# Scores of the first units moved to other PSUM banks, and the opening's instruction list rewritten around it

## The chip, the cores and the metric

The kernel runs on one core of a Trainium2 chip. The metric is the time of one execution on the device, in microseconds (us); lower is better. The engines are PE (matrix multiply), DVE (vector), ACT (scalar, activation functions), POOL (GpSimd) and SP, which here only starts DMA transfers. Each engine takes its own instructions in the order in which they were issued.

## What is computed

Windowed attention feeds a feed-forward layer whose gate is a softmax. The inputs are `q`, `k`, `v` of 8 batches, 8 heads, 576 positions and 64 columns, in fp32:

```python
scores = q @ k.T / 8
# heads 0-3: the last 32 positions; heads 4-7: every 4th of the last 128
scores = where(mask, scores, -1e9)
attn = exp(scores - max); attn /= sum(attn) + 1e-9
x = (attn @ v) as (4608 tokens, 512)
h = x @ w_in                       # 512 -> 1024
solu = h * softmax(h)
ln = (solu - mean) / sqrt(var + 1e-6) * g_ln
out = ln @ w_out                   # 1024 -> 512
```

`w_in` and `w_out` arrive as fp64 and are turned into fp32 on the chip.

## The kernel before

**Attention** works on 32 units n, each a pair of heads of one batch. `q` and `v` load a unit. `S` makes the scores: two matmuls that put the mask down and 80 small ones (lines 203, 211). Then `max`, `sub`, `exp`, `sum`, `inv`, `norm` make the softmax (lines 237 to 268), `turn` transposes it on DVE (L273), `V` multiplies with v (L289), and `xh`, `xl` split the result into two parts of reduced precision, `x_hi` and `x_lo` (L314, L328; on POOL, L322, a copy `xc`, L318, comes out of PSUM first). `sub` is on DVE (L247) straight out of PSUM, except for the units in `ACT_SCORES`: there ACT copies the scores out (`cp`, L241) and POOL subtracts (L250). `norm` runs on POOL for the units in `POOL_NORM`, else on DVE (both L268); `xl` runs on POOL for the units in `POOL_X`.

**The feed-forward part** works on 36 tiles i of 128 tokens. The product h is made in four quarters of 6 matmuls, `ha hb hc hd` (L341): `ha` and `hb` give the first 512 columns, `hc` and `hd` the second, and `ha`, `hc` need the first half of the 512 inputs (the first two units of a batch), `hb`, `hd` the others. Then `peak` (DVE, L352), `e` (ACT, L359), `gate` (DVE, L366), `mid` (ACT for tiles in `ACT_CENTRE`, L379, else DVE, L382) and `var` (ACT and six small POOL instructions). `forth` and `back` carry the tile through DRAM, `trA trB` transpose on DVE (L455), `thA thB` (ACT) and `tlA tlB` (POOL, L468) split it, `o` multiplies with `w_out` (24 matmuls, L477), and `out` scales and stores.

**The weights** come in 16 parts b, 0 to 7 of `w_in` and 8 to 15 of `w_out`: `w` loads one (512 KB), `abs` and `low` (ACT), `clamp` (DVE, L519), `sign` (DVE, L526) and `join` (DVE, L534) build the fp32 number, `gain` scales it (`w_out` only), `hi` (ACT, L544) and `lo` (L548) split it; `lo` is on DVE for the parts in `DVE_LOW`, else on POOL. `ha` needs parts 0 and 2, `hc` 1 and 3, `hb` 4 and 6, `hd` 5 and 7.

**PSUM** is one tensor of 8 banks of 512 columns. h of tiles 0 and 2 lies in banks 0 and 1, h of all other tiles in banks 2 and 3, `o` in bank 0 or 1, the result of `V` in columns 0 to 143 of banks 4 to 7. Scores of units below `MERGED` lie in banks 2 and 3, those of the others in columns 144 to 463 of banks 6 and 7. Waits are derived by the framework from what each instruction reads and writes.

**The order** is written out by hand: `OPENING` is one list of words, each word issues one step, and it reaches to tile 7 and unit 11. After it a loop issues the words of `STEP` for each tile. An engine's queue is the list's words that belong to it, in the list's order. SP's words are `w q v ib m g i forth back`. A transfer into a buffer waits for the last reader of what was there (`w7` for `sign0`, `q4` for S0, `v6` for V2).

PE's order in the opening before: S0 S1 S2 V0 S3 V1 S4 V2 ha1 hc0 V3 ha0 hb0 S5 hd0 hc1 V4 hb1 hd1 S6 ha2 hc2 V5 hd2 hb2 hc3 S7 ha3 hb3 hd3 V6 S8 hc4 V7 ha4 hd4 hb4 S9 o0 hc5 ha5 hd5 hb5 o1 V8 and so on.

Of the kernel before, what the change touches and what calls it, by code (L numbers as in the profile page):

```python
# [28 lines left out]
WQ = 2 * WIN  # L29
NG = P // WIN  # L30
GQ = S // NG
NS = -(-GQ // WIN)
# [4 lines left out]
SIGN_BIT = -(1 << 31)  # L37
PE_MASK = (0, 1, 2, 3, 4, 5, 6, 7, 8, 9)
POOL_SUB = True
POOL_NORM = (0, 1, 2, 3, 4, 5, 6, 7, 8, 9)  # L40
ACT_SCORES = (1, 5, 7, 8, 9)
POOL_X = (0, 4, 5)
DVE_LOW = (12, 13, 14, 15)
ACT_CENTRE = (0, 1, 2, 3, 4)
Q_BUFS, V_BUFS, T_BUFS, TH_BUFS, CONV_BUFS = 4, 4, 4, 2, 4
REBIAS = 2.0**16
F64_MIN = REBIAS * float(np.array(0x38000000, np.uint32).view(np.float32))
F64_MAX = REBIAS * float(np.array(0x47EFFFFF, np.uint32).view(np.float32))
FIRST = 6
OPENING = (  # L50
# [25 lines left out]
)  # L76
STEP = (
    "back.j trA.k thA.k trB.k thB.k tlA.k tlB.k ha.i hb.i S.n q.n mask.n max.n sub.n hc.i hd.i "
# [8 lines left out]
BY_PE = "t.i th.i tl.i".split()  # L87
LAST = NTILE - 1
SLOTS = "t0 t1 t2 t3 raw4 raw5 tp t0 t1 t2 t3 raw4 raw5 tp t3 tp".split()
MERGED = 5  # L90
SHIFT = {"th0": 88}


# [1 line left out]
def windowed_attention_then_solu_kernel(  # L95
# [41 lines left out]
    banks = psum.tile([P, 8, 512], F32, name="banks")  # L137
# [8 lines left out]

    def ps_s(n):
        if n < MERGED:
            return banks[:, 2:4, 0 : NS * WQ]
        return banks[:, 6:8, GQ : GQ + NS * WQ]  # L150

    nc.vector.memset(mhalf, -0.5)
# [41 lines left out]
    def scores(n):  # L194

        qt, kt = loaded[n]["q"], loaded[n]["k"]
        dil = int(n % NPAIR >= NPAIR // 2)
        ps = ps_s(n)
        st[n] = {"ps": ps.rearrange("p h (s w) -> p h s w", w=WQ)}
        on_pe = n in PE_MASK  # L200
        if on_pe:
            for h in range(2):
                nc.tensor.matmul(  # L203
                    out=ps[:, h, :], lhsT=id_bf, rhs=mask_sb[:, dil, :],
                    start=True, stop=False, skip_group_check=True,
                )
        for i in range(NS):
            for h in range(2):
                for c in range(NG):
                    q0 = GQ * c + WIN * i  # L210
                    nc.tensor.matmul(  # L211
                        out=ps[WIN * c : WIN * c + WIN, h, WQ * i : WQ * i + WQ],
                        lhsT=qt[D * h : D * h + D, q0 : q0 + WIN],
                        rhs=kt[D * h : D * h + D, q0 : q0 + WQ],
                        start=not on_pe,
                        stop=True,
                        skip_group_check=True,
                    )

    def soft_mask(n):  # L220
        if n in PE_MASK:
            return
        dil = int(n % NPAIR >= NPAIR // 2)
        sm = st[n]["sm"] = att.tile([P, 2, NS, WQ], F32, name=f"sm{n % 2}")
        nc.vector.tensor_tensor(  # L225
            out=sm.rearrange("p h s w -> p h (s w)"), in0=ps_s(n),
            in1=mask_sb[:, dil, :].unsqueeze(1).broadcast_to([P, 2, NS * WQ]),
            op=ALU.add,
        )

    def wide(x):
        return x.unsqueeze(3).broadcast_to([P, 2, NS, WQ])
# [10 lines left out]
    def soft_sub(n):  # L243
        mx = st[n]["mx"]
        if n in PE_MASK and n not in ACT_SCORES:
            sm = st[n]["sm"] = att.tile([P, 2, NS, WQ], F32, name=f"sm{n % 2}")
# [18 lines left out]
    def soft_norm(n):  # L265
        sm, rs = st[n]["sm"], st[n]["rs"]
        eng = nc.gpsimd if n in POOL_NORM else nc.vector
        eng.tensor_tensor(out=sm, in0=sm, in1=wide(rs), op=ALU.mult)  # L268
# [51 lines left out]
    def spread_lo(n):  # L320
        if n in POOL_X:
            nc.gpsimd.tensor_tensor(  # L322
                out=x_part(n, x_lo), in0=st[n]["x"], in1=x_part(n, x_hi).bitcast(F32),
                op=ALU.subtract,
            )
            del st[n], loaded[n]
            return
        nc.vector.tensor_tensor(  # L328
            out=x_view(n, x_lo), in0=from_v(n), in1=x_view(n, x_hi).bitcast(F32), op=ALU.subtract
        )  # L330
        del st[n], loaded[n]
# [39 lines left out]
    def moe_centre(i):  # L371
        src, dst, mu = ms[i]["t"], ms[i]["t"], ms[i]["mu"]
        if not by_dma(i):
            ms[i]["t"] = moe.tile([P, DF], F32, name="tp", bufs=1)
            dst = ms[i]["t"].rearrange("p (k j s) -> p k j s", j=NG, s=WIN)
            src = src.rearrange("p (j k s) -> p k j s", j=NG, s=WIN)
        if i in ACT_CENTRE:
            nc.vector.tensor_scalar(out=mu, in0=mu, scalar1=-1.0 / DF, scalar2=None, op0=ALU.mult)
# [167 lines left out]
    def conv_lo(b):  # L546
        eng = nc.vector if b in DVE_LOW else nc.gpsimd
        eng.tensor_tensor(  # L548
            out=w_part(b)[:, 1, :], in0=cv[b]["mag"], in1=hi(b).bitcast(F32), op=ALU.subtract
        )  # L550
        del cv[b]
# [30 lines left out]
    for i in range(FIRST, NTILE + 2):  # L582
        of = {"n": fronts.get(i), "m": fronts.get(i - 1), "i": i, "j": i - 1, "k": i - 2}
        words_of = {LAST: LAST_STEP}.get(i, STEP)
        for word in (words_of if i <= LAST else "o.k out.k").split():
            name, which = word.split(".")
            n = of[which]
# [78 lines left out]
```

## Time and profile before

| what | value |
|---|---|
| runs shown | 519.17, 519.04, 516.50 us (median 519.04) |
| profiled execution | 515.99 us, of which the span from first to last instruction is 514.2 |
| granted clock of PE | 0.998 |
| busy: PE, DVE, ACT, POOL | 482.4, 343.0, 235.2, 218.5 us |
| first matmul of h | 40.65 us |
| DMA | 88.37 MB, mean 172 GB/s |

In the profile's lists a line such as L341 is the line of the kernel that issued the instruction; "x12" is a count; "[1.66 <-DVE x_lo L328]" says that the engine stood idle for 1.66 us and that the DVE instruction of line 328 which writes `x_lo` ended it. The stretches give, for each engine, busy microseconds in that stretch and the number of instructions. Neighbouring instructions of one engine overlap a little in the records, so the chain, which cuts them to what follows on, gives the shorter and better durations.

### The profile page before, as it was taken

What the parts mean: (1) busy time and instruction counts of PE and PEld (TensorE: products, weight loads), DVE (VectorE), ACT (ScalarE), POOL (GpSimd) and SP (SyncE); (2) the same over time, 40 slices, a digit from 0 to 9 for tenths busy, and PEclk for the clock granted to TensorE, in tenths of its full rate; (3) what the DMA queues carried; (4) which work ended last, traced back from release to release, by engine and by line L of the source; (5) the groups of instructions that cost most, each with busy time, mean ns of one, the idle gap of its engine ahead of it and who ended that gap; (6) DMA issues with size and microseconds to landing.
All of it is one profiled execution on the core that took longest, in us unless ns stands there. A gap on an engine that the chain in (4) does not pass through costs nothing.

```text
span 514.2 us, 16377 instructions
## 1 busy us (share of the span) xinstructions
PE 482.4 (94%) x7132; PEld 388.2 (75%) x7132; DVE 343.0 (67%) x539; ACT 235.2 (46%) x387; POOL 218.5 (42%) x342
## 2 busy tenths in 40 slices
PE   1359989999999999999999999999999999999997
PEld 1237767788788888888888888888877888888885
DVE  3999999766467765577677766576677776444540
ACT  3857888633344443344433344343434444333351
POOL 1634775634444443444434443444444334333360
PEclk9999999999999999999999999999999999999999
DMA  7969186636585664556655564646644333333331
GB/s 274 402 234 376 46 286 197 197 125 212 169 273 184 184 180 137 153 183 182 182 169 172 181 182 137 183 154 184 177 141 134 105 106 91 111 108 103 108 98 61
DMA packets 47304, 88.37 MB, mean 172 GB/s; under 512 B 5504, under 2 KB 23808, under 8 KB 47232
## 3 DMA queue, kind: packets, MB, share of 16 engines
q1 hardware_dynamic: 47232, 87.32, 53.2%
q8 instruction: 56, 0.92, 0.7%
q14 instruction: 16, 0.13, 0.1%
HBM read 59.51 MB, written 27.79 MB: 170 GB/s over the span
## 4 chain that ended last, share of the span: by engine, by line
PE 90%; DMA 4%; DVE 3%; SPq 1%; issue 0%; ACT 0%; ACTq 0%; DVEq 0%
PE banks L341 40%; PE banks L477 39%; PE banks L289 6%; PE banks L211 5%; DMA raw<-w_in 1%; DMA kt<-kT 1%; DMA qt<-qT 1%; DVE low L526 1%; DVE pt L273 0%; DVE mag L534 0%; DVE rs L258 0%; PE banks L203 0%; DVE sm L247 0%; DVE mx L237 0%; SPq L165 0%
## 5 line engine op out<-in xcount | busy, mean ns | idle before, releaser
L341 PE MATMUL banks<-w_i,x_hi 128*128 128x512 f32 x576 | 183.1, 399 | 0.5 <-DVE mu L366 0.4
L477 PE MATMUL banks<-w_o,th 128*128 128x512 f32 x576 | 181.0, 395 | 0.0
L341 PEld LDWEIGHTS banks<-w_i,x_hi 128*128 128x128 f32 x576 | 106.6, 190 | 24.6 <-DVE mu L366 1.0
L477 PEld LDWEIGHTS banks<-w_o,th 128*128 128x128 f32 x576 | 106.2, 188 | 22.1 <-DVE w_o L548 0.2
L341 PE MATMUL banks<-w_i,x_lo 128*128 128x512 f32 x288 | 113.0, 393 | 0.0
L477 PE MATMUL banks<-w_o,tl 128*128 128x512 f32 x288 | 112.2, 390 | 0.0
L468 POOL TENSOR_TENSOR tl<-t,th 128x512 fp32r<-128x512 f32 x70 | 89.7, 1299 | 41.1 <-ACT th L463 41.1
L352 DVE TENSOR_REDUCE nmax<-banks 128x1 f32<-128x1024 f32 x36 | 44.0, 1223 | 65.2 <-PE banks L341 65.2
L254 ACT ACTIVATE sm<-sm 128x640 f32<-128x640 f32 x32 | 23.5, 736 | 94.5 <-POOL sm L250 94.0
L359 ACT ACTIVATE e<-banks,nmax 128x1024 f32<-128x1024 f32 x36 | 40.2, 1117 | 51.4 <-DVE nmax L352 50.8
L341 PEld LDWEIGHTS banks<-w_i,x_lo 128*128 128x128 f32 x288 | 54.5, 189 | 11.7
L477 PEld LDWEIGHTS banks<-w_o,tl 128*128 128x128 f32 x288 | 54.1, 188 | 11.7
L387 ACT ACTIVATE e<-t 128x1024 f32<-128x1024 f32 x35 | 37.2, 1062 | 55.2 <-DVE t L382 55.2
L366 DVE CUSTOM_DVE_ANT_0 t<-banks,e 128x1024 f32<-128x1024 f32 x36 | 43.9, 1219 | 17.1 <-ACT e L359 17.0
L289 PEld LDWEIGHTS banks<-pt,vt 32*64 32x64 f32 x2816 | 34.8, 138 | 18.9 <-issue 11.3
L463 ACT CAST th<-t 128x512 fp32r<-128x512 f32 x70 | 41.7, 619 | 15.9 <-DVE t L455 8.6
L455 DVE STREAM_TRANSPOSE t<-raw 128x512 f32<-128x512 f32 x70 | 44.9, 677 | 3.8 <-issue 2.6
L225 DVE TENSOR_TENSOR sm<-banks,mask_sb 128x640 f32<-128x640 f32 x22 | 18.1, 824 | 44.0 <-PE banks L211 43.8
L250 POOL TENSOR_TENSOR sm<-sm,mx 128x640 f32<-128x640 f32 x27 | 34.5, 1276 | 29.7 <-DVE mx L237 26.7
L289 PE MATMUL banks<-pt,vt 32*64 32x64 f32 (+3 forms) x2816 | 38.1, 234 | 7.7 <-DVE pt L273 7.7
L392 POOL TENSOR_SCALAR sq<-sq 128x1 f32<-128x1 f32 x36 | 7.7, 215 | 86.1 <-ACT e L387 85.6
L388 POOL TENSOR_SCALAR se<-se 128x1 f32<-128x1 f32 x36 | 8.7, 243 | 77.3 <-ACT e L359 76.6
(62 smaller groups left out, 474.7 us busy)
## 6 DMA issues: line engine op xcount, KB each, us to landing
mid<-t SPq DMA_DIRECT2D x140, 128.0 KB, 2.3
raw<-mid SPq DMA_DIRECT2D x35, 512.0 KB, 3.5
vt<-vw SPq DMA_DIRECT2D x32, 384.0 KB, 4.0
kt<-kT SPq DMA_DIRECT2D x32, 312.0 KB, 4.2
qt<-qT SPq DMA_DIRECT2D x32, 296.0 KB, 4.6
out<-ob SPq DMA_DIRECT2D x36, 256.0 KB, 2.1
t<-w_in SPq DMA_DIRECT2D x5, 512.0 KB, 7.2
t<-w_out SPq DMA_DIRECT2D x4, 512.0 KB, 6.7
```

Source lines behind the costliest of these rows:

```text
L211: nc.tensor.matmul(out=ps[WIN * c : WIN * c + WIN, h, WQ * i : WQ * i + WQ], lhsT=qt[D * h : D * h + D, q0 : q0 + WIN], rhs=kt[D * h : D * ...
L250: eng.tensor_tensor(out=st[n]["sm"], in0=st[n]["sm"], in1=wide(mx), op=ALU.subtract)
L289: nc.tensor.matmul(out=ps_x[D * h : D * h + D, c, c0 : c0 + k1 - k0], lhsT=vt[WIN * c : WIN * c + WIN, i, D * h : D * h + D], rhs=pt[WIN * ...
L341: nc.tensor.matmul(out=ps_h(i)[:, half], lhsT=a[:, kt, xs], rhs=w_i[:, kt, half, part, :], start=(kt == 0 and k == 0), stop=(kt == KT - 1 ...
L352: nc.vector.tensor_reduce(out=nmax, in_=h, axis=AX.X, op=ALU.max, negate=True)
L359: nc.scalar.activation(out=e, in_=h, func=AF.Exp, bias=nmax, scale=1.0, accum_out=se)
L366: nc.vector.tensor_tensor_reduce(out=t, in0=h, in1=ms[i]["e"], scale=1.0, scalar=0.0, op0=ALU.mult, op1=ALU.add, accum_out=mu,)
L387: nc.scalar.activation(out=e, in_=t, func=AF.Square, accum_out=sq)
L455: nc.vector.transpose(out=turned(i)[:, cut(c)].rearrange("p k (a r) -> p k a r", r=WIN), in_=ms[i]["mv"].rearrange("p (a k s) -> p k a s", ...
L463: nc.scalar.copy(out=ms[i]["th"][:, cut(c)], in_=turned(i)[:, cut(c)])
L468: nc.gpsimd.tensor_tensor(out=ms[i]["tl"][:, cut(c)], in0=turned(i)[:, cut(c)], in1=ms[i]["th"][:, cut(c)].bitcast(F32), op=ALU.subtract,)
L477: nc.tensor.matmul(out=ps_o(i), lhsT=a[:, f, :], rhs=w_o[:, f, part, :], start=(f == 0 and k == 0), stop=(f == FT - 1 and k == 2),)
```

## The change

`MERGED` goes from 5 to 4, and the units below it no longer share one pair of banks: units 0 and 2 keep banks 2 and 3, units 1 and 3 use banks 0 and 1. Unit 4 joins the later units in banks 6 and 7.

The lists that share work among engines change, and so does the whole opening list, which keeps all steps that it had but for a few at its far end that the loop issues instead.

```diff
-POOL_NORM = (0, 1, 2, 3, 4, 5, 6, 7, 8, 9)
-ACT_SCORES = (1, 5, 7, 8, 9)
-POOL_X = (0, 4, 5)
-DVE_LOW = (12, 13, 14, 15)
-ACT_CENTRE = (0, 1, 2, 3, 4)
+POOL_NORM = (0, 1, 2, 3, 4, 5, 6, 7)
+ACT_SCORES = (5, 6, 9)
+POOL_X = (1, 4, 5, 6)
+DVE_LOW = (7, 9, 11, 12, 15)
+ACT_CENTRE = (0, 1, 2, 4, 5)
...
-    "w1 ib abs1 w3 m0 low1 q0 clamp1 w0 sign1 w2 abs3 q1 low3 q2 join1 hi1 S0 sign3 clamp3 "
-    "join3 hi3 w4 low0 max0 sub0 m1 sign0 abs0 w5 S1 clamp0 abs2 low2 w8 exp0 lo1 join0 clamp2 "
...
+    "ib m0 q0 w1 S0 low1 q1 w2 max0 w0 m1 abs1 sub0 exp0 low2 low0 q2 sign1 clamp1 w5 sum0 w3 "
+    "abs2 v1 S1 abs0 inv0 join1 v0 hi1 max1 norm0 sub1 exp1 abs3 clamp2 sign2 turn0 low3 sum1 "
+    "lo1 inv1 sign0 join2 S2 w4 clamp0 clamp3 abs5 sign3 join3 q3 V0 q4 max2 S3 sub2 clamp5 "
+    "norm1 hi3 join0 w6 xh0 turn1 exp2 xl0 lo3 hi2 V1 sum2 hi0 low5 inv2 low4 lo0 low6 v2 abs4 "
+    "sign4 sign5 clamp4 join4 join5 max3 w7 norm2 w8 xc1 xh1 xl1 low7 sub3 turn2 S4 exp3 lo2 "
+    "hi5 q6 sum3 inv3 abs7 abs6 max4 hc1 w12 sub4 norm3 sign6 V2 ha0 hi4 clamp6 w9 join6 hc0 "
...
-MERGED = 5
+MERGED = 4
...
         if n < MERGED:
-            return banks[:, 2:4, 0 : NS * WQ]
+            return banks[:, 2:4, 0 : NS * WQ] if n % 2 == 0 else banks[:, 0:2, 0 : NS * WQ]
         return banks[:, 6:8, GQ : GQ + NS * WQ]
```

On SP the new list starts ib m0 q0 w1 q1 w2 w0 m1 q2 w5 w3 v1 v0 w4 q3 q4 w6 v2 w7 w8 q6 w12 w9 w10 v3 g v5 v4 v6 w11 q5 v7 w14 q7 forth0 q9 back0 forth1 w13 q8 v8 back1 w15 forth2.

PE's order in the new opening: S0 S1 S2 V0 S3 V1 S4 hc1 V2 ha0 hc0 V3 ha1 hb0 S5 hd0 hd1 V4 hb1 S6 hc2 ha2 hb2 V5 hd2 S7 hc3 ha3 V6 hb3 hd3 V7 S8 ha4 hc4 hb4 hd4 S9 hc5 hd5 ha5 hb5 o0 o1 ha6 hc6 hb6 hd6 V8 and so on.

DVE's order in the new opening up to its fifth `gate`: max0 sub0 sign1 clamp1 sum0 inv0 join1 max1 sub1 clamp2 sign2 turn0 sum1 inv1 sign0 join2 clamp0 clamp3 sign3 join3 max2 sub2 clamp5 join0 turn1 xl0 sum2 inv2 sign4 sign5 clamp4 join4 join5 max3 sub3 turn2 sum3 inv3 max4 sub4 sign6 clamp6 join6 clamp7 turn3 xl2 sum4 sign7 join7 clamp10 xl3 inv4 sign10 lo7 join10 clamp8 max5 peak0 turn4 sign11 sign8 gate0 sum5 inv5 peak1 max6 clamp11 join11 turn5 gate1 sign14 sum6 join8 peak2 inv6 max7 sub7 turn6 sign9 sum7 inv7 gate2 turn7 trA0 peak3 clamp9 xl7 join9 gate3 trB0 mid3 lo9 clamp14 sign13 max8 sub8 sign12 peak4 clamp12 join12 gate4.

42 rows, old and new, of the table OPENING are left out of this document.

## Prediction

> **What bounds the kernel now.** I read the page first, then the busy time by stretches, the waits of PE, the chain that ended last, and the timelines of PE, DVE and POOL up to 110 us.
>
> ```profile
> span 514.2 us, 16377 instructions
> PE 482.4 (94%) x7132; PEld 388.2 (75%) x7132; DVE 343.0 (67%) x539; ACT 235.2 (46%) x387; POOL 218.5 (42%) x342
> ```
> ```profile
> core 0: us, PE busy (x) PEld busy (x) DVE busy (x) ACT busy (x) POOL busy (x), PEclk, DMA share, GB/s
> 10.20:40.65 30.45, 14.33 (x680) 11.17 (x680) 30.01 (x47) 18.67 (x31) 16.76 (x13) 1.00 0.88 333
> 40.65:60.00 19.35, 19.35 (x391) 14.94 (x392) 18.00 (x27) 15.94 (x26) 9.85 (x8) 1.00 0.54 207
> 60.00:92.45 32.45, 30.01 (x596) 22.98 (x595) 30.50 (x50) 27.38 (x44) 21.05 (x34) 1.00 0.72 232
> 92.45:140.00 47.55, 47.55 (x539) 38.75 (x540) 31.43 (x52) 20.92 (x35) 25.33 (x36) 1.00 0.53 163
> ```
>
> PE bounds the kernel as a whole: from 92.45 us on it does not pause. What a change of the opening list can move lies ahead of that. Up to 40.65 us PE works less than half the time while DVE is busy for 30.01 of 30.45 us. From 40.65 to 92.45 us both are nearly full. So the opening is paced by the DVE queue, and an earlier PE start is kept only if DVE's work for it is ready earlier too.
>
> ```profile
> PE banks L289 <- DVE pt L273: 7.7, 4, 3.6
> PE banks L203 <- DVE sm L247: 5.7, 2, 3.2
> PE banks L203 <- DVE x_lo L328: 1.7, 1, 1.7
> PE banks L341 <- DVE mu L366: 0.4, 1, 0.4
> ```
> ```profile
> 40.65 4.95 PE banks L341 x12
> 46.61 2.99 PE banks L341 x12
> ...
> 68.99 4.32 PE banks L341 x18
> ...
> 86.63 5.80 PE banks L477 x24
> 92.45 5.73 PE banks L341 x24
> 98.18 5.44 PE banks L477 x24
> ```
> ```profile
> 39.09 1.49 PE L289 MATMUL banks<-pt,vt 32*64 32x64 f32 x80 [1.61 <-DVE pt L273]
> ...
> 76.00 0.43 PE L203 MATMUL banks<-mask_sb,id_bf 128*128 128x320 bf16 x2 [1.66 <-DVE x_lo L328]
> ...
> 77.82 0.73 PE L341 MATMUL banks<-w_i,x_hi 128*128 128x512 f32 x2 [0.41 <-DVE mu L366]
> ```
>
> All those waits end on DVE. The first is for `turn`. The second is `S` waiting until `sub` of the unit before has emptied banks 2 and 3. The third shows that banks are guarded whole: S8 writes columns 144 to 463 of banks 6 and 7, yet waits for `xl6`, which reads columns 0 to 143. The last is tile 4 waiting for `gate3`.
>
> **The change, part by part.** The unit of account is DVE's progress up to `gate4`, because in both lists hc5 may not start before it (tiles 4 and 5 share banks 2 and 3), and little else on PE is left to cover it.
>
> ```profile
> 10.23 0.69 DVE L526 SCALAR_TENSOR_TENSOR low<-t,low 128x512 int32<-128x512 int32 x1 [2.65 <-ACT low L513]
> ...
> 20.87 1.75 DVE L526 SCALAR_TENSOR_TENSOR low<-raw,low 128x512 int32<-128x512 int32 x1
> ...
> 91.16 1.22 DVE L366 CUSTOM_DVE_ANT_0 t<-banks,e 128x1024 f32<-128x1024 f32 x1 [0.30 <-ACT e L359]
> ```
>
> *Before:* DVE runs almost without a pause from 10.23 us (`clamp1 sign1 join1` done) to the end of `gate4` at 92.39; hc5 starts at 92.45, with o0 already done.
>
> *Start.* The new SP list sends the 720 KB of ib, m0 and q0 ahead of w1. The row below is `abs3`, released by w3, whose end was 1056 KB into the old list. w1's end is now 1232 KB in; at the 333 GB/s of the stretch row or more, that is at most half a microsecond later, 9.4. Its `low1` gives `sign1` at 10.1, with `max0 sub0` done instead of three weight steps of the same length. Start: -0.1.
>
> ```profile
> 8.90 0.66 ACT L503 ACTIVATE mag<-t 128x512 f32<-128x512 f32 x1 [2.77 <-DMA t<-w_in]
> ```
>
> *Order and engines.* I counted DVE's words ahead of `gate4` in both lists. The new one has two `clamp`, three `join`, one `sign`, two `lo` and one `xl` fewer; two `sub` and one `mid` (unit 1 and 8, tile 3) more. Durations, as pieces of the chain (the last three from DVE's timeline):
>
> ```profile
> 31.06 0.60 DVE low L526
> 31.66 0.60 DVE mag L534
> 32.27 0.34 DVE mag L519
> ...
> 34.66 0.73 DVE sm L247
> ```
> ```profile
> 47.38 0.76 DVE L328 TENSOR_TENSOR x_lo<-banks,x_hi 128x576 fp32r<-128x576 f32 x1
> ...
> 88.97 1.89 DVE L548 TENSOR_TENSOR w_o<-mag,w_o 128x512 fp32r<-128x512 f32 x3
> ...
> 102.91 0.85 DVE L382 TENSOR_SCALAR t<-t,mu 128x1024 f32<-128x1024 f32 x1
> ```
>
> -2 x 0.34 - 3 x 0.60 - 0.60 - 2 x 0.63 - 0.76 + 2 x 0.73 + 0.85 = -2.8. Norms of units 8 and 9 move to DVE only behind `gate4`, where DVE has 16 us of slack (31.43 of 47.55 busy): nothing. Copies `cp1 cp7 cp8 xc0` leave ACT, `cp6 xc1 xc6` come: nothing, ACT was idle 12 of 30 us before 40.65.
>
> *Stretch by POOL.* `sign`, `join` and `clamp` sometimes take over a microsecond longer. The 1.75 us `sign4` above ran beside this POOL instruction and ended half a microsecond behind it:
>
> ```profile
> 20.36 1.71 POOL L268 TENSOR_TENSOR sm<-sm,rs 128x640 f32<-128x640 f32 x1
> ```
>
> The sum of it is mean less median, times count:
>
> ```profile
> L534 DVE SCALAR_TENSOR_TENSOR mag<-mag,low 128x512 int32<-128x512 int32 x16 | 12.7, 801 | 0.2
> ...
> L526 DVE SCALAR_TENSOR_TENSOR low<-t,low 128x512 int32<-128x512 int32 x9 | 9.6, 1073 | 2.9 <-ACT low L513 2.9
> L519 DVE TENSOR_SCALAR mag<-mag 128x512 f32<-128x512 f32 x16 | 8.7, 549 | 4.6 <-ACT mag L503 4.6
> ...
> L526 DVE SCALAR_TENSOR_TENSOR low<-raw,low 128x512 int32<-128x512 int32 x4 | 3.8, 949 | 0.0
> L526 DVE SCALAR_TENSOR_TENSOR low<-tp,low 128x512 int32<-128x512 int32 x3 | 3.1, 1044 | 0.0
> ```
> ```profile
> L534 DVE SCALAR_TENSOR_TENSOR mag<-mag,low x16: 630/683/1635, 6.9 to 86.6; 128x512 int32<-128x512 int32 x16
> ```
> ```profile
> L526 DVE SCALAR_TENSOR_TENSOR low<-t,low x9: 684/691/1910, 6.2 to 55.5; 128x512 int32<-128x512 int32 x9
> ```
> ```profile
> L519 DVE TENSOR_SCALAR mag<-mag x16: 365/418/1496, 5.5 to 84.5; 128x512 f32<-128x512 f32 x16
> ```
>
> 12.7 + 16.5 + 8.7, less 16 x 0.683, 16 x 0.691 and 16 x 0.418, is 9.2 us. Ahead of `gate4` the new list has 14 `clamp`, 15 `sign`, 13 `join` and 2 `lo` on DVE, 44 where there were 16, 16, 16 and 4, 52; and on POOL 25 long words (9 `lo`, 8 `norm`, 2 `sub`, 4 `xl`, 2 `tl`) for 29 (12, 8, 4, 3, 2). 9.2 x 44/52 x 25/29 = 6.7, so -2.5. Where they meet cannot be read from the old trace; the ends are an unchanged stretch (0) and one more than halved (-5.5). I take the middle, since both lists mix the two engines alike.
>
> The Trainium skill, SBUF — State Buffer, section "SBUF: two separate sides", says why: the pair of ports that both engines use is an exclusive lock held for the whole instruction. The rows agree: the loser waits for the end. By that rule in its worst form, each of `sign5 clamp4 join4` would wait out a whole `norm2`, `xl1` or `lo2`; that is the slower rival below.
>
> *The banks.* Units 1 and 3 in banks 0 and 1 take S1 and S3 off `sub0` and `sub2`. This removes the 5.7 us of the second wait row, but PE then waits for `turn` and for q1 instead, so alone it gives nothing. Unit 4 in banks 6 and 7 adds two waits: S4 behind `xh1 xc1`, V2 behind `max4 sub4`, with ha0 hc0 V3 queued behind V2 on PE. The cover is hc1, which now stands ahead of V2: 6 matmuls, 1.5 us of the 2.99 row. DVE's queue prices this. Before, `sub4` ended as the first L341 matmul began, at 40.65, 30.4 us behind 10.23. Up to `sub4` the new list has two `clamp`, `sign` and `join` each fewer and one `sub` more, -2.35: it ends at 10.1 + 30.4 - 2.35 = 38.1 with the stretch of before, and near 35.5 with half of the 5 us that I put to this part. So V2 starts between 35.5 and 38.1, against 39.09, with one quarter of tile 1 already done; it costs DVE nothing by itself.
>
> By the Trainium skill, TensorE: Matmul & The Clock Gate, section "What's actually happening", an idle window halves the clock until the array has been busy again. The trace has 4.95 us for the first 12 matmuls and 2.99 for the next, though the granted clock reads 1.00 for both. The rule then makes hc1 and, behind V2's wait, ha0 and hc0 slow, 2 us more ahead of V3; by it alone the sum would stay as it is, since DVE is the later of the two there.
>
> *Waits of DVE.* Between 10.20 and 92.45 DVE was not busy for 0.44 + 1.35 + 1.95 = 3.7 us (stretch rows), about 1 us of it in gaps too small to be a wait. In the new list I can name 1.75: `sum0` behind exp0 0.25, `clamp2` behind abs2 0.2, `xl3` behind V3 and `xh3` 1.0, `gate4` behind e4 0.3 as in the row at 91.16. With the same small gaps that is 2.7: -1.0. The ends are no wait (-2.7) and some that I do not see (+4, the slower rival).
>
> *SP.* q5 stands behind v6, which must wait for V2's end; then w11 and q5 follow. 384 + 512 + 608 KB at 333 GB/s is 4.6 us, and S5 stands 7 us behind V2 (four quarters, twice the 2.99 row, and V3): covered, if the start of the transfers takes less than 2.4 us. w15 now waits for `sign13` with forth2 behind it; `trA2` is late enough. The other queue moves are behind free slots.
>
> *Sum.* `gate4` ends at 92.39 - 0.1 - 2.8 - 2.5 - 1.0 = 86.0. hc5 follows 0.06 behind. But o0 is not yet done: the new list has it behind hb5, because the weights `lo11` to `lo15` come later. That leaves 5.44 us more on PE than before at the same point: 86.0 + 0.06 + 5.44 - 92.45 = **-0.95 us**. Between hd4 and hc5 PE has only S9 (1.4 us) against the 4.5 us that hd3's end (73.3, row at 68.99) to 77.82 took with V6 and S8 between them; this stall is in the number. Behind hc5, h5, o0 and o1 cover everything as in the last stretch.
>
> The profiled execution took 515.99 us (span 514.2); the runs shown have a median of 519.04, 3.05 above it. -0.95 makes the profiled execution 515.0 and the median **518.1 us**.
>
> **The rivals.**
> - *Faster.* The POOL instructions fall beside DVE's reductions and transposes and the stretch drops by 5.5 instead of 2.5: `gate4` at 83.0, -3.95 us, 515.1. For it: DVE need do four weight steps fewer ahead of `turn1`, V1 comes some 4 us sooner, ACT and POOL have less to do. Against it: the saved time comes from order alone. 0.36.
> - *Slower.* S4's new banks put V2 behind `sub4`, and POOL's `norm2 xl1 lo2` meet `sign5 clamp4 join4`, each meeting costing the 1.1 us of the 1.75 row. V2 then starts at 39.1 (38.1 and one meeting more than before), ends at 40.7; ha0 and hc0 take 4.95 us as the first twelve matmuls did, V3 ends near 46.7 and `xl3` near 48.1, where it ended before (row at 47.38). The words from there to `gate4` differ by 0.7 us, the stretch behind it by some 1.4: `gate4` at 90.3, +3.35 us, 522.4. It decides when V2 starts later than 38. For it: 1.66 us were lost the same way at S8. Against it: the words that must be done ahead of V2 are fewer. 0.23.
> - *The new placement does nothing*: waits on `sub` become waits on `turn`, DVE's order evens out. That is the forecast's neighbourhood: 0.41 within 0.5% (2.6 us), about what can be told here.
>
> **How the numbers follow.** The forecast's own range is 516.4 to 521. Both signs hold much of the rest, so the range reaches to 513.5 (the faster case with the rest of DVE's named waits gone) and 522 (the slower one without its last half microsecond); about one in ten lies beyond each end. Faster 0.36, same 0.41, slower 0.23.
>
> **What the profile would show.** `gate4` (fifth L366) ending near 86, hc5 right behind it after a PE pause of 2 to 3 us, o0 later than h5; the first L341 matmul near 31 us, followed by a pause ended by `sub4` (L247); stretched L526, L534 and L519 down to about 6.7 us in sum; no PE pause behind o0. The prediction is wrong if POOL and DVE meet much more or less than in proportion, if PE pauses behind o0, or if q5 or w15 comes late.

## The result and the profile after

The changed kernel takes 521.81 us (median of 20 runs, 518.71 to 525.46), the kernel before 516.93 beside it (20 runs, 514.74 to 521.99): 1.0089 of before, 95% interval 1.0071 to 1.0108, slower by 3.7 to 5.6 us. The profiled execution took 520.29 us, of which the span is 518.5, 4.3 more than before. Its page:

```profile
span 518.5 us, 16380 instructions
PE 485.9 (94%) x7132; PEld 388.9 (75%) x7132; DVE 344.2 (66%) x543; ACT 234.8 (45%) x386; POOL 214.8 (41%) x338
```

As many matmuls as before keep PE busy 3.5 us longer (485.9 against 482.4), so most of the 4.3 us is booked as work, not as waiting. Its mean granted clock is 0.992 instead of 0.998, but not all of the 3.5 us is the clock: the lines of `S` (L211) have 36.5 us instead of 35.2, of which 1.2 lie in S2, S3 and S8, where a pause cuts the 80 matmuls in two, and those of h (L341) have 1.0 us more. Here are PE's waits, all of them after and, in the second fence, those of before that the prediction did not show:

```profile
PE banks L211 <- DMA qt<-qT: 5.7, 4, 2.6
PE banks L203 <- DMA mask_sb<-mask: 4.6, 2, 3.3
PE banks L211 <- issue: 4.0, 3, 2.7
PE banks L341 <- DVE mu L366: 2.7, 1, 2.7
PE banks L289 <- issue: 2.6, 1, 2.6
PE banks L289 <- DMA vt<-vw: 2.5, 1, 2.5
PE banks L203 <- DVE x_lo L328: 1.5, 1, 1.5
PE banks L289 <- DVE pt L273: 1.4, 1, 1.4
PE banks L203 <- ACT x_hi L314: 1.3, 1, 1.3
PE banks L477 <- POOL tl L468: 1.0, 1, 1.0
PE banks L412 <- DVE tp L382: 0.9, 1, 0.9
PE banks L341 <- issue: 0.6, 1, 0.6
```
```profile
PE banks L203 <- DMA mask_sb<-mask: 9.2, 1, 9.2
...
PE banks L203 <- ACT sm L241: 2.4, 1, 2.4
...
PE banks L211 <- DMA qt<-qT: 0.9, 1, 0.9
```

The waits that the change aimed at went: 5.7 us for `sub` and 7.7 for `turn` became 0 and 1.4, the mask's 9.2 became 4.6. What took their place: 5.7 us for queries (0.9 before), 2.5 for a v, 2.7 ahead of hc5, and 7.2 us that end on "issue", where the profile shows nothing that PE waited for and of which before has none. The sums are 28.8 after and 28.0 before. The early start was given back in full.

Two places on PE's timeline show slow matmuls behind a pause, and the third pause shows none; then two pauses late in the program:

```profile
51.53 1.20 PE L289 MATMUL banks<-pt,vt 32*64 32x32 f32 x96 [1.39 <-DVE pt L273]
52.66 1.07 PE L341 MATMUL banks<-w_i,x_hi 128*128 128x512 f32 x2
...
74.95 0.43 PE L203 MATMUL banks<-mask_sb,id_bf 128*128 128x320 bf16 x2 [1.52 <-DVE x_lo L328]
75.31 0.62 PE L211 MATMUL banks<-kt,qt 64*32 64x64 f32 x37
76.70 0.91 PE L211 MATMUL banks<-kt,qt 64*32 64x64 f32 x43 [0.76 <-issue]
77.54 1.22 PE L341 MATMUL banks<-w_i,x_hi 128*128 128x512 f32 x2
...
88.50 0.73 PE L341 MATMUL banks<-w_i,x_hi 128*128 128x512 f32 x2 [2.73 <-DVE mu L366]
...
138.92 0.50 PE L477 MATMUL banks<-w_o,tl 128*128 128x512 f32 x1 [0.99 <-POOL tl L468]
...
502.80 1.09 PE L412 MATMUL banks<-id_sb,tp 128*128 128x128 f32 x8 [0.86 <-DVE tp L382]
```

The first two h matmuls behind V4 and S8 take 1.07 and 1.22 us instead of 0.73. The clock records of the trace give the reason. They begin at 35.79 us; from there on each slow stretch ahead of the program's end lasts 3.41 us at half the clock, and all changes of the clock are multiples of 3.41 us apart, as on a grid. Stretches cut on that grid (the seventh column is the granted clock):

```profile
49.45:52.86 3.41, 2.02 (x101) 1.53 (x100) 3.41 (x5) 2.81 (x6) 2.48 (x2) 1.00 0.45 167
52.86:56.27 3.41, 3.41 (x37) 2.01 (x40) 3.31 (x8) 2.60 (x4) 1.72 (x2) 0.50 0.02 5
73.34:76.75 3.41, 1.13 (x55) 0.72 (x50) 3.41 (x7) 3.06 (x7) 3.00 (x5) 1.00 0.36 141
76.75:80.16 3.41, 3.41 (x49) 2.76 (x49) 3.37 (x7) 3.41 (x7) 0.81 (x1) 0.50 0.02 5
83.57:86.98 3.41, 2.19 (x87) 1.43 (x85) 2.25 (x3) 1.12 (x3) 0.76 (x2) 1.00 0.89 264
86.98:90.40 3.42, 1.90 (x8) 1.59 (x9) 3.16 (x7) 3.00 (x5) 0.00 (x0) 1.00 0.59 204
```

The grid cuts the 2.73 us ahead of hc5 in two, and neither half is followed by a slow stretch. In w4, an experiment below, the same wait of 2.73 us lies within one stretch of that trace's grid, and the slow clock follows:

```profile
85.46:88.87 3.41, 0.68 (x21) 0.47 (x9) 2.96 (x8) 2.67 (x5) 0.00 (x0) 1.00 0.93 327
88.87:92.28 3.41, 3.41 (x10) 2.64 (x9) 3.41 (x8) 3.38 (x6) 0.00 (x0) 0.50 0.12 38
```

So what counts is how a pause falls on the grid, and the grid lies elsewhere in the program in each trace. PE's busy time alone does not decide it: 2.02 us with V4's small matmuls was followed by a slow stretch, 1.90 us ahead of and in hc5 was not. In before the clock records begin at 44.83 us. The 1.00 that the views print ahead of that is no reading, so it does not speak against a slow clock under the first 12 matmuls of h (40.65 us on), as the prediction took it to.

DVE's timeline shows what h4's lateness does: `peak4` (L352) waits for it, and `gate4` (L366) follows.

```profile
84.54 1.22 DVE L352 TENSOR_REDUCE nmax<-banks 128x1 f32<-128x1024 f32 x1 [1.96 <-PE banks L341]
...
87.21 1.23 DVE L366 CUSTOM_DVE_ANT_0 t<-banks,e 128x1024 f32<-128x1024 f32 x1 [0.38 <-ACT e L359]
```

### The profile page after: what moved, and what is told of

It reads as the page before. It is cut to its first block, busy times and chain, and to the rows that moved or that the text cites. A ratio compares the mean times of both kernels' runs of the same rounds, so it can differ in the third digit from the quotient of the medians.

```text
span 518.5 us, 16380 instructions
## 1 busy us (share of the span) xinstructions
PE 485.9 (94%) x7132; PEld 388.9 (75%) x7132; DVE 344.2 (66%) x543; ACT 234.8 (45%) x386; POOL 214.8 (41%) x338
## 4 chain that ended last, share of the span: by engine, by line
PE 70%; DVE 9%; DMA 9%; issue 3%; ACT 3%; SPq 3%; POOL 1%; DVEq 0%; ACTq 0%
PE banks L477 31%; PE banks L341 29%; PE banks L289 5%; PE banks L211 4%; DMA qt<-qT 3%; DMA raw<-mid 2%; DMA mid<-t 2%; SPq L439 2%; DMA kt<-kT 1%; DVE low L526 1%; DVE t L366 1%; DVE t L455 1%; DVE nmax L352 1%; DMA tp<-w_out 1%; DVE mx L237 1%
## 5 line engine op out<-in xcount | busy, mean ns | idle before, releaser
L341 PE MATMUL banks<-w_i,x_hi 128*128 128x512 f32 x576 | 183.6, 400 | 2.7 <-DVE mu L366 2.7
L341 PEld LDWEIGHTS banks<-w_i,x_hi 128*128 128x128 f32 x576 | 106.7, 190 | 26.5 <-DVE mu L366 2.9
L341 PE MATMUL banks<-w_i,x_lo 128*128 128x512 f32 x288 | 113.5, 394 | 0.6 <-issue 0.6
L352 DVE TENSOR_REDUCE nmax<-banks 128x1 f32<-128x1024 f32 x36 | 43.8, 1218 | 63.7 <-PE banks L341 63.7
L341 PEld LDWEIGHTS banks<-w_i,x_lo 128*128 128x128 f32 x288 | 54.6, 190 | 13.4 <-issue 1.4
L366 DVE CUSTOM_DVE_ANT_0 t<-banks,e 128x1024 f32<-128x1024 f32 x36 | 43.9, 1220 | 19.5 <-ACT e L359 19.5
L211 PEld LDWEIGHTS banks<-kt,qt 64*32 64x32 f32 x2560 | 30.2, 113 | 22.5 <-issue 15.4
L211 PE MATMUL banks<-kt,qt 64*32 64x64 f32 x2560 | 36.5, 240 | 9.7 <-DMA qt<-qT 5.7
L250 POOL TENSOR_TENSOR sm<-sm,mx 128x640 f32<-128x640 f32 x25 | 32.0, 1280 | 32.8 <-DVE mx L237 31.1
```

The costliest lines, as they stand in the source:

```text
L211: nc.tensor.matmul(out=ps[WIN * c : WIN * c + WIN, h, WQ * i : WQ * i + WQ], lhsT=qt[D * h : D * h + D, q0 : q0 + WIN], rhs=kt[D * h : D * ...
L250: eng.tensor_tensor(out=st[n]["sm"], in0=st[n]["sm"], in1=wide(mx), op=ALU.subtract)
L341: nc.tensor.matmul(out=ps_h(i)[:, half], lhsT=a[:, kt, xs], rhs=w_i[:, kt, half, part, :], start=(kt == 0 and k == 0), stop=(kt == KT - 1 ...
L352: nc.vector.tensor_reduce(out=nmax, in_=h, axis=AX.X, op=ALU.max, negate=True)
L366: nc.vector.tensor_tensor_reduce(out=t, in0=h, in1=ms[i]["e"], scale=1.0, scalar=0.0, op0=ALU.mult, op1=ALU.add, accum_out=mu,)
```

## The experiments

Ratios are to the kernel before, run beside each, with 95% intervals. Where an experiment's list is one line shorter, the line numbers behind it are one lower (L340 for L341). The theories: A, hc5 waiting for `gate4` through banks 2 and 3; B, the early loads that stall TensorE; C, the new banks themselves; D, a pause that costs twice, as a wait and as slow matmuls behind it; E, DVE's pace; F, the late transpose of tile 3.

**Places and loads: A, B, C, F.**

```diff
e1_h4_banks01:  return banks[:, 0:2] if i in (0, 2, 4) else banks[:, 2:4]
e2_hb1_first:   ... e0 turn4 sign11 w14 sub5 sign8 exp5 lo10 hb1 V4 gate0 ...
e3_banks_only:  list and engines of before, with the new ps of units 0 to 4
e4_late_loads:  ... turn3 v3 w8 q6 hi6 ...      (both stood ahead of V2)
e5_trA3_early:  ... trB3 trA3 forth5 ...
```

> The changed kernel with one more edit: h of tile 4 goes to banks 0 and 1 (of tile 2) instead of 2 and 3, so that tiles 3, 4 and 5 no longer follow one another in the same two banks. Theory A (the lead of about 5 us that the new list has at S5 is given back in three pauses of PE, at V4, at S8 and at hc5, and in the slow matmuls behind the first two): hc5 no longer waits for gate4, its pause of 2.73 us goes, and the ratio to the kernel before falls from 1.009 to about 1.004 (-2.7 us). Theory B (the loss is early: PE waits for blocks of its own instructions while the loads fill the DMA queues, 2.71 us inside S3 and 2.55 us inside V1, and all later work is late by that): the pause at hc5 turns into another one of the same length and the ratio stays near 1.009. Theory C (S4 in banks 6 and 7 costs it): no change, 1.009.

> The changed kernel with hb1 moved ahead of V4 in PE's order. Theory A: the pause of 1.39 us at V4 is filled, the slow matmuls at 52.7 to 55.9 us (granted clock 0.72 to 0.86) run at full clock, 1.6 us more; peak1 is earlier. If all of it is kept, -3 us, ratio 1.003; if DVE is late for S8 and hc5 anyway, those pauses grow and the ratio stays above 1.006. Theory B and C: less than 1 us, 1.008 to 1.009.

> The kernel before, with its own list and engines, and only the banks of the scores changed as in the changed kernel (units 1 and 3 in banks 0 and 1, unit 4 in banks 6 and 7). Theory C: slower by 3 to 5 us, ratio 1.006 to 1.009, with V2 behind sub4 and S4 behind the copies of unit 1. Theory A and B: the new list makes the loss, and this kernel lies within 0.3% of the one before (S1 is free earlier, V2 later; DVE paces both).

> The changed kernel with the loads w8 and q6 (1.1 MB) moved behind v3 on SP, so that the DMA queues are not full while S3, V1 and S4 run. Theory B: the pauses inside S3 and V1 (5.3 us together) shrink below 1.5 us, V1 ends 2.5 us earlier, and the whole kernel gains 2 to 4 us, ratio 1.001 to 1.005. Theory A: the pauses shrink in the same way, but DVE paces this part (it waits for it only 0.78 us), so the ratio falls by 0.002 at most, to 1.007 or more.

> The changed kernel with trA3 moved ahead of turn8 on DVE, so that it no longer stands behind gate6: the buffer that back5 waits for is free 9 us earlier, and o5 need not wait for tl5. Theory F (behind hc5 the new list has a wait of its own, 0.99 us of L477 for tl, because back5 is late): this pause goes, ratio down by 0.002 to 1.007. Rival (tl5 is late for another reason, v12 and q10 ahead of back5 on SP): the pause stays.

Measured: e1 1.0089 [1.0061, 1.0118]; e2 1.0097 [1.0063, 1.0131]; e3 1.0014 [0.9993, 1.0035]; e4 1.0098 [1.0062, 1.0134]; e5 1.0106 [1.0069, 1.0143]. None but e3 differs from the changed kernel. e3 clears the banks: the loss comes with the new list and the new sharing among engines, which no run takes apart. The others took a wait away and got another, or left it. PE's timeline of e1, e2 and e4, in that order:

```profile
93.34 0.50 PE L477 MATMUL banks<-w_o,th 128*128 128x512 f32 x1 [0.23 <-ACT w_o L544]
94.99 0.50 PE L477 MATMUL banks<-w_o,th 128*128 128x512 f32 x1 [1.15 <-POOL w_o L548]
97.07 0.50 PE L477 MATMUL banks<-w_o,th 128*128 128x512 f32 x1 [0.86 <-POOL w_o L548]
98.87 0.80 PE L477 MATMUL banks<-w_o,th 128*128 128x512 f32 x1 [0.82 <-DVE w_o L548]
```
```profile
56.80 0.43 PE L202 MATMUL banks<-mask_sb,id_bf 128*128 128x320 bf16 x2 [1.28 <-ACT x L317]
66.34 0.43 PE L202 MATMUL banks<-mask_sb,id_bf 128*128 128x320 bf16 x2 [1.14 <-ACT x_hi L313]
```
```profile
47.65 1.03 PE L210 MATMUL banks<-kt,qt 64*32 64x64 f32 x80 [1.70 <-DMA qt<-qT]
```

In e1 the 2.73 us ahead of hc5 are gone, and o0 waits 0.23 + 1.15 + 0.86 + 0.82 = 3.06 us for its weights instead: A names a wait that is there, but removing it alone is worth nothing; that another would take its place is what B had foretold of this run. In e2 V4's pause is gone and S6 and S7 pause. In e4 V1's pause without a wait falls from 2.55 to 0.91 us, S3's stays (2.73 us), and S5 waits 1.70 for its late query, so this run takes away only a part of B's stall, and that did not pay. e5 leaves the pause at 138.92 (139.14 there, 0.99 us): F is refuted; its rival, the transfer of `back5`, was not tried.

**DVE's pace: E.** Both kernels without the sign step of the `w_out` parts (the sign is left out of the weights).

```diff
     def conv_sign(b):
+        if b >= 8:
+            return
```

> The changed kernel without the sign step of the weight parts 8 to 15 (left out: the sign of w_out): eight DVE instructions of 0.6 us or more less, 5 to 7 us, all ahead of o0. Theory E (DVE paces the new list from S5 to o0, so the lead of 5 us that PE has at S5 is lost to DVE): the kernel gains 2.5 to 5 us, ratio 0.999 to 1.004. Rival (PE's own pauses and clock make the loss): less than 1 us, ratio above 1.007.

> The kernel before without the sign step of the weight parts 8 to 15 (left out: the sign of w_out). Theory E: PE has only 2.7 us of pauses in this kernel between 40.65 us and the end, so it gains 2 us at most, ratio 0.996 to 1.000. Rival: it gains as much as the changed kernel does, or more.

Measured: w2 1.0067 [1.0033, 1.0101], w3 0.9983 [0.9966, 1.0]. Eight sign steps (5 us or more of DVE) are worth about 1 us in each. w2's interval reaches into E's range (up to 1.004) and over the rival's bound (1.007), so the times alone do not settle it. DVE's timeline of w2 says more: with less to do, DVE waits for h4 longer than the 1.96 us of the changed kernel.

```profile
85.84 1.22 DVE L352 TENSOR_REDUCE nmax<-banks 128x1 f32<-128x1024 f32 x1 [4.21 <-PE banks L341]
```

There it is PE that is late; DVE's pace is not what sets the two kernels apart.

**The clock: D.** Unread matmuls are put where PE pauses, so that it stays busy; nothing else changes.

```diff
+    def keep_warm(k):
+        bank, count = ((4, 6), (0, 8), (1, 12))[k]
+        for _ in range(count):
+            nc.tensor.matmul(
+                out=banks[:, bank, GQ : GQ + NS * WQ], lhsT=id_bf, rhs=mask_sb[:, 0, :],
+                start=True, stop=True, skip_group_check=True,
+            )
w1_warm, w11_fill_three:  6 ahead of V4, 8 ahead of S8, 12 ahead of hc5 (as above)
w4_behind_pauses:         6 behind V5, 8 behind hb4, 12 behind o0
w6: 8 ahead of S8;  w8: 6 ahead of V4;  w9: 12 ahead of hc5;  w7: w8 and w9
w5: 4 ahead of S4, 6 of V4, 5 of S7, 8 of S8, 16 of hc5;  w10: w5 without S4's
b1: before with 8 ahead of S4, 4 ahead of V2, 8 ahead of S8
```

> The changed kernel with matmuls added whose output nobody reads, in PE's order ahead of V4 (6), of S8 (8) and of hc5 (12), each 128 x 320, into free columns: the pauses are filled with work, nothing is made ready earlier. Theory D (a pause costs twice: PE runs its matmuls at half speed behind it, 0.43 us for 0.23, and behind S8 no other engine is late, so the 1.3 us lost in h4 reach gate4 and hc5): the slow L341 rows at 52.7 and 77.5 us go, hc5 starts 1.3 us earlier, ratio 1.005 to 1.007 although PE does more. Rival (DVE alone sets gate4): no gain, ratio 1.009 or above, as the added 26 matmuls (about 4.5 us of PE) fill time that PE had anyway or cost some.

> The changed kernel with the same 26 unread matmuls as in the kernel that filled the pauses ahead of V4, S8 and hc5, but at places where TensorE does not pause: 6 behind V5, 8 behind hb4 and 12 behind o0. Theory D (a pause costs twice, as a wait and as slow matmuls behind it): the work now comes on top, 26 x 0.14 = 3.6 us, of which the pauses ahead of S8 and hc5 swallow up to 2; the pauses themselves and the slow rows behind V4's and h4's start stay; ratio 1.011 to 1.016, at least 0.006 above the kernel that filled the pauses (1.0029). Rival (the 26 instructions helped because they shifted the blocks in which instructions arrive, or merely delayed TensorE): the place does not matter, ratio 1.001 to 1.005.

> The changed kernel with 8 unread matmuls ahead of S8 only. Theory D, if S8's pause is the one that counts (it is the last ahead of gate4, and h4 behind it ran 1.3 us slow): ratio 1.003 to 1.006, half of the gain or more. If V4's or hc5's pause counts instead: 1.008 to 1.010. If each is worth the same share of the 3 us: about 1.007.

> The changed kernel with 39 unread matmuls in five pauses: 4 ahead of S4, 6 ahead of V4, 5 ahead of S7, 8 ahead of S8, 16 ahead of hc5. Theory D: at most 1.0029, perhaps 1.000 to 1.002, since S4's and S7's pauses are filled too. Rival (what was won came from one place only, and more unread work is only more work): 1.004 to 1.008.

> The kernel before with 20 unread matmuls in its own pauses: 8 ahead of S4, 4 ahead of V2, 8 ahead of S8. Theory D as a rule for both kernels: its first matmuls behind the pause at S4 and V2 run at the slow clock (12 of them take 4.95 us instead of 2.99), so the filling gains 1 to 2.5 us of 517: ratio 0.995 to 0.998. Rival (there VectorE sets the pace at gate4, and TensorE's clock does not count until then): 0.999 to 1.002; slower than 1.002 if the unread matmuls run into the scores' banks' way.

> The changed kernel with 6 unread matmuls ahead of V4 and 12 ahead of hc5, none ahead of S8. Over the 20 runs of the changed kernel the span fell by 0.53 us for each 0.001 of mean granted clock (0.987 to 0.997). Theory D with V4's and hc5's pauses as the ones that count: mean clock over its runs 0.997 or more, ratio 1.002 to 1.005, as with all three filled (1.0029). Rival (only the three together do it, or the one good result was luck): clock 0.990 to 0.995, ratio 1.007 to 1.010.

> The changed kernel with 6 unread matmuls ahead of V4 alone. If V4's pause is the one that slows the clock: mean clock 0.996 or more, ratio 1.002 to 1.006. If hc5's is: 1.008 to 1.010 and the clock near 0.991, as in the changed kernel. If both count by halves: 1.006.

> The changed kernel with 12 unread matmuls ahead of hc5 alone. If hc5's pause (2.73 us) is the one that slows the clock: mean clock 0.996 or more, ratio 1.002 to 1.006. If V4's is: 1.008 to 1.010 and the clock near 0.991; the profile of the changed kernel speaks for this, its rows behind hc5's pause being at full speed.

> The changed kernel with 35 unread matmuls in four pauses: 6 ahead of V4, 5 ahead of S7, 8 ahead of S8, 16 ahead of hc5; that is the kernel with five fills without its 4 ahead of S4. Theory D, with the loss of the five put down to S4's place: mean clock 0.998 or more, ratio 1.001 to 1.004. Rival (five fills lost because more unread work is more work): 1.005 to 1.008 at the same clock.

> The three fills again (6 ahead of V4, 8 ahead of S8, 12 ahead of hc5), on the chip of the run beside it. Theory D, the three together: mean clock 0.998 or more and ratio 1.001 to 1.005, below all singles (1.0087 and 1.0088). Rival (the first result was that chip's): ratio 1.006 to 1.009.

| kernel | ratio [95%] | mean clock of its runs | mean span, us |
|---|---|---|---|
| before (96 runs beside the others) | 1 | 0.9950 | 515.4 |
| changed (20 runs) | 1.0089 [1.0071, 1.0108] | 0.9912 | 520.2 |
| w6, S8 | 1.0088 [1.0061, 1.0115] | 0.9967 | 519.5 |
| w8, V4 | 1.0087 [1.006, 1.0115] | 0.9943 | 520.1 |
| w9, hc5 | 1.0088 [1.007, 1.0106] | 0.9947 | 520.1 |
| w7, V4 and hc5 | 1.0062 [1.0039, 1.0086] | 0.9955 | 518.4 |
| w1, three | 1.0029 [1.0011, 1.0048] | 0.9993 | 517.0 |
| w11, three again | 1.0068 [1.0045, 1.0091] | 0.9983 | 518.2 |
| w10, four | 1.0079 [1.0054, 1.0105] | 0.9990 | 518.5 |
| w5, five | 1.0075 [1.0044, 1.0105] | 0.9979 | 519.2 |
| w4, same work elsewhere | 1.0132 [1.0107, 1.0158] | 0.9928 | 521.8 |
| b1, before filled | 0.9989 [0.9968, 1.0009] | 0.9954 | 514.8 |

Over the 20 runs of the changed kernel the span falls by 0.53 us for each 0.001 of mean clock (correlation -0.86), from 522.5 at 0.987 (6 runs) to 518.1 at 0.995 and more (6 runs); 0.001 of 486 us of PE work is 0.49. Over the 96 of before it falls by 0.12: there, as far as the profiles of w3 and b1 show it (slow stretches at 31.8 to 45.5 and 40.0 to 43.4 us), the slow matmuls lie ahead of waits on DVE that can hide them. Carried on to a clock of 1.0, which none of its runs had, the changed kernel's line ends at 515.5; the 19 runs of before at 0.998 or more have 514.8. By that reckoning some 4 of the 4.7 us between the means go with the clock. It is a fit over runs and no proof of cause: a longer pause may set both, and the profiles below speak against a share that large.

The fills are the test. PE's timeline of w11 at the two places:

```profile
54.21 0.72 PE L340 MATMUL banks<-w_i,x_hi 128*128 128x512 f32 x2
...
78.30 0.73 PE L340 MATMUL banks<-w_i,x_hi 128*128 128x512 f32 x2
```

With the pauses filled w11's clock reads 1.00 from 54 to 58 and from 78 to 82 us, and the h matmuls behind them take 0.72 and 0.73 us. hc5 then starts at 88.05, 0.45 us earlier, not the 1.3 expected. w1's one profile, of its slowest execution (521.51 us), still has a slow stretch behind S8 (79.98 to 83.39 us).

By the ratios the kernel is 1.1 us (w11) to 3.1 us (w1) faster than the changed one although PE has 26 matmuls more to do, about 3.9 us (the six ahead of V4 took 0.91 in w11); the same 26 at places without a pause (w4) cost 2.2 us. So the place decides, and the rival of shifted instructions falls.

But D missed most of its sizes: no single fill won anything that can be told, V4's and hc5's together won 1.4 us, five and four fills (w5, w10) only 0.5 to 0.7 at the clock of w1, S4's four matmuls not being the reason, and w11 lies where the rival put it (the first result may be partly that chip's); its interval overlaps the changed kernel's.

Three profiles (w11, w10, w5) have no slow stretch ahead of the program's end; their spans are 517.7, 517.2 and 521.0 us, still 3.0 to 6.8 above the 514.2 of before. So the slow clock is one cause, seen in the rows and worth 1.1 to 1.4 us where it can be followed (next section); it does not account for the whole.

w6 shows why S8's own fill is worth nothing. Its timeline:

```profile
75.88 0.44 PE L210 MATMUL banks<-kt,qt 64*32 64x64 f32 x29
77.99 1.06 PE L210 MATMUL banks<-kt,qt 64*32 64x64 f32 x51 [1.67 <-issue]
78.98 1.22 PE L340 MATMUL banks<-w_i,x_hi 128*128 128x512 f32 x2
```

S8's wait is filled, but the pause without a wait inside S8 grows from 0.76 to 1.67 us, h4 is as slow as before, and hc5 still waits 2.74. b1 tested little: the runs' clock stayed at 0.995, and its time is that of before. No version here beats before beyond its interval.

**The pauses without a wait.**

```diff
+    def tiny(_):
+        for _ in range(127):
+            nc.tensor.matmul(
+                out=banks[0:1, 6, GQ : GQ + 1], lhsT=id_bf[:, 0:1], rhs=id_bf[:, 0:1],
+                start=True, stop=True, skip_group_check=True,
+            )
i1_shift_count:  ... m0 q0 w1 tiny0 S0 ...
```

> The changed kernel with 127 unread matmuls of one column ahead of S0, where TensorE waits for the first mask, so that each later matmul stands 127 places further on. If the pauses without a wait are set by the count (they stood at the matmuls 190, 444, 698, 952 and 1208 of the list, 254 apart), they move 127 matmuls of the list forward: none at S3's matmul 5 or V1's matmul 52 in the old place, but at 317, 571, 825 and 1081. Rival (they are set by what these places read or by a transfer): S3 still pauses 2.7 us after 5 matmuls and V1 after 52. Time: 1.005 to 1.011, since the 127 take up to 6 us, most of it under the wait for the first mask and the first query.

Measured: 1.008 [1.0052, 1.0107]. Each pause stands one matmul further on in the list (S8's after 38 instead of 37). The expectation had the distance wrong: 254 counts weight loads with matmuls. PE's timeline of the changed kernel has from one pause to the next 75 matmuls of S3 and 52 of V1, 127:

```profile
25.35 1.36 PE L211 MATMUL banks<-kt,qt 64*32 64x64 f32 x75 [2.71 <-issue]
26.64 1.19 PE L289 MATMUL banks<-pt,vt 32*64 32x32 f32 x52
30.38 0.95 PE L289 MATMUL banks<-pt,vt 32*64 32x64 f32 x44 [2.55 <-issue]
```

So 127 more are nearly a whole period, and this run cannot tell the theories apart. The fills do: S8's pause stands after 37 matmuls in the changed kernel and after 29 with 8 more ahead of it (w6, above); with 14 more ahead (w1) after 23:

```profile
77.25 0.42 PE L210 MATMUL banks<-kt,qt 64*32 64x64 f32 x23
78.86 0.80 PE L210 MATMUL banks<-kt,qt 64*32 64x64 f32 x57 [1.18 <-issue]
```

The count of PE's instructions sets the place, and the records show why: instructions arrive in blocks, and these pauses end on one. The page lists a DMA queue of the kind `instruction`, q8, with 56 packets of 16 KB; 7132 matmuls and as many weight loads are 255 for each packet, and i1, with 127 matmuls more, has 57, 255 for each again. In the trace of the changed kernel the five pauses end at 16.32, 25.35, 30.38, 36.41 and 76.70 us, each 1.3 to 1.5 us after such a packet ended (15.00, 24.00, 28.96, 34.96, 75.32). All 91 pauses on "issue" that PE has in the 20 traces end 1.2 to 1.6 us behind one. What makes a packet come too late is not shown: the DMA engines are 0.93 busy from 9.59 to 34.55 us, around the first four, but only 0.36 from 73.34 to 76.75, around the fifth. By themselves the pauses need not cost: e3 has 4.3 us of them at a ratio of 1.0014.

## Why the prediction was wrong

*Start, list, stretch* held: `sign1` began at 9.59 (10.1 forecast), and from there to the end of `gate4` DVE was busy for 73.38 us, where before it was 78.45 from 10.23: 5.1 less, 2.8 + 2.5 forecast. Over the whole program L526, L534 and L519 took 15.3 + 12.8 + 6.9 us, 6.3 above their counts at the medians of before (6.7 forecast). The faster rival fell here: it needed a stretch 5.5 us smaller, and it became 2.9 smaller.

*The banks* held, and the slower rival's mechanism did not occur: `sub4` ended at 37.08, V2 began at 37.53, inside 35.5 to 38.1. The first L341 came at 34.55 instead of 31, because S3 and V1 had paused 2.7 and 2.55 us without a wait, and no pause for `sub4` followed. q5 and w15 were not late.

*Waits of DVE* is the term that failed. It was -1.0 us, 2.7 of waits in all. The stretches after show 1.31 + 0.56 + 3.63 = 5.5 us in which DVE was not busy (0.03 of them behind `gate4`):

```profile
9.59:34.55 24.96, 12.00 (x518) 8.91 (x518) 23.65 (x38) 15.56 (x26) 10.30 (x8) 1.00 0.93 364
34.55:60.00 25.45, 23.36 (x486) 17.08 (x482) 24.89 (x39) 19.30 (x31) 14.67 (x16) 0.93 0.62 203
60.00:92.45 32.45, 27.43 (x580) 21.21 (x579) 28.82 (x50) 25.87 (x43) 16.86 (x28) 0.95 0.50 150
```

That is +1.8 instead of -1.0, and `gate4` ended at 88.44, 2.4 behind the 86.0 forecast. The wait that the prediction did not name is the 1.96 us of `peak4` for h4. It is as long as the pause inside S8 (0.76) and what h4's first six matmuls lost (2.69 us where w11's took 1.50) together. Four profiles of the same list, with fills or without, show what it is worth. The last column runs from hc5's start to the end of the span; before has 427.2 there with o0's 5.44 added.

| profile | S8 starts | `gate4` ends | between | slow clock on h4 | pause inside S8 | from hc5 on |
|---|---|---|---|---|---|---|
| changed | 74.95 | 88.44 | 13.49 | yes | 0.76 | 430.0 |
| w11 | 75.93 | 88.00 | 12.07 | no | 0.87 | 429.6 |
| w10 | 75.74 | 87.17 | 11.43 | no | none | 430.0 |
| w5 | 79.17 | 90.60 | 11.43 | no | none | 430.3 |

The slow clock is worth 1.4 us on this path and the pause 0.6. Five more profiles with a slow stretch on h4 (w1, w6, w9, i1, e5) agree: what their time between has beyond 11.43 us and their own pause inside S8 is 1.1 to 1.4 us. With neither, `gate4` would have ended at 74.95 + 11.43 = 86.4 us, by this estimate, near the forecast. S8's start itself differs by up to 4.2 us among the four; w5, the latest, has 10.7 us of pauses without a wait, w10 has 5.2.

*The clock rule.* The prediction said that by the Trainium skill (TensorE: Matmul & The Clock Gate, "What's actually happening") the sum would stay as it is, since DVE is the later of the two. Further on than V3, PE and DVE wait for each other in turn (V4 for `turn4`, S8 for `xl7`, `peak4` for h4), and there a slow matmul goes straight into the sum. The same section of the Trainium skill has the clock fall after an idle window of about 3.4 us. The trace differs: slow rows followed a pause of 1.39 us, and pauses of 1.52 and 0.76 us close together. Behind the 2.73 us ahead of hc5 the first two matmuls took 0.73 us here, full speed, but 0.86 in w4, 0.96 in w8 and 1.22 in w2. The section of the Trainium skill calls the window free-running, by which the phase would decide; the grid of 3.41 us that lies elsewhere in each trace agrees, and so do the changed kernel's clocks of 0.987 to 0.997 from run to run.

*Ahead of hc5* the pause of 2.73 us was as foretold. With hc5 at 88.50 the sum becomes 88.50 + 5.44 - 92.45 = +1.5 us.

*"Behind hc5, h5, o0 and o1 cover everything"* was wrong: 0.99 at 138.92 and 0.86 at 502.80, 1.85 us more. 1.5 + 1.85 = 3.35 of the 4.3 us. Of the last 0.95, 0.85 is PE busy time behind hc5 (424.32 us against 418.03 and o0's 5.44), at a clock of 1.00, in no single row. The table shows that this part does not depend on the clock: w10, whose hc5 starts at 87.24 and so lies only 0.2 us behind before, loses its other 2.8 us there. The 0.86 comes and goes (none in w11, 0.8 in w10), and its cause is open. The 0.99 stands in every profile of the changed list, and DVE's and POOL's timelines show where it comes from:

```profile
131.69 0.71 DVE L455 STREAM_TRANSPOSE t<-raw 128x512 f32<-128x512 f32 x1 [4.20 <-DMA qt<-qT]
135.87 1.77 POOL L250 TENSOR_TENSOR sm<-sm,mx 128x640 f32<-128x640 f32 x1 [3.00 <-DVE mx L237]
137.60 2.52 POOL L468 TENSOR_TENSOR tl<-t,th 128x512 fp32r<-128x512 f32 x2
```

By the list's order these are `trB6`, `sub11`, and `tlA5 tlB5`: o5 waits for `tlA5`, which stands on POOL behind `sub11`, which waits for `max11`, which stands on DVE behind `trB6`, which waits for a transfer. The prediction did not follow POOL's queue behind hc5. That another order would save the 0.99 us was not tried.

*The range.* The measured 521.81 us lies inside 513.5 to 522 and close to the slower rival's 522.4. That is luck: the rival's chain (V2 late behind `sub4`, POOL meeting DVE) did not happen, and the forecast had the kernel faster.

What stays open: why w1 and w11, the same program, lie at 1.0029 and 1.0068; why fills that bring the clock to 0.999 do not bring the whole 4 us that the fit over runs promises; and what the new sharing among engines costs by itself.

## What to carry to other kernels

When a wait on one engine is taken away, add up all idle time of the bounding engine before and after by releaser: here 16.6 us of waits for `sub`, `turn` and the mask went, and the sum rose by 0.8. Then compare the busy time of the same instructions, and the mean clock, run by run: a kernel whose waits hide a slow clock may lose by moving the waits. A pause that ends on nothing the profile shows can be set against the packets of the instruction queue. Where two engines feed each other in turn, no stall is hidden because one of them was the later on average.

## What the hardware showed that was not expected

The granted clock fell to a half for 3.41 us, or for twice that (w2, w7, w8), behind pauses of 1.4 us and of 1.5 + 0.8; behind one of 2.7 us it fell in some profiles (w2, w4, w8) and not in others (changed, w6). All its changes in one trace lie on a grid of 3.41 us that lies elsewhere in the next. 26 unread matmuls in the pauses changed the time by -1.1 us (inside the intervals) and -3.1, the same at other places by +2.2. PE's pauses without a wait, 0.2 to 3.7 us each, stand at fixed counts of its instructions, 127 matmuls apart where two follow each other, move with inserted ones, and end 1.2 to 1.6 us after a 16 KB packet of the instruction queue.
